# T5-bias attention into a bilinear feed-forward block on one NeuronCore: a reordered start of the queues, value rows of 160 bytes, and five more pairs of outputs transposed by DMA

## The chip, the cores and the metric

The kernel runs on one core of a Trainium2 chip. The metric is the device time of one execution in microseconds, as the median of several executions. A NeuronCore has five engines that each run their own instructions in order: TensorE (PE in the profile, its weight loads PEld), VectorE (DVE), ScalarE (ACT), GpSimd (POOL) and SyncE (SP), which here issues DMAs only. DMAs are issued by SP, ACT and GpSimd and run on the core's 16 DMA engines.

## The reference

```python
# q, k, v: 8 batches x 8 heads x 576 x 64, float32; bias_table: 32 buckets x 8 heads
scores = scale * np.matmul(q, k.transpose(0, 1, 3, 2))        # scale = 1/8
n = np.abs(pos[:, None] - pos[None, :])
bucket = np.where(n < 16, n, min(31, 16 + int(log(n / 16) / log(128 / 16) * 15)))
scores = scores + bias_table[bucket].transpose(2, 0, 1)
attn = softmax(scores);  y = attn @ v
x = y.transpose(0, 2, 1, 3).reshape(4608, 512)
out = ((x @ w_a) * (x @ w_b)) @ w_out                         # 512 -> 1536 -> 512
```

(The bucket's line is shortened here to one formula.) From a distance of 128 on all positions have bucket 31, so only a band around the diagonal has a bias that differs from a constant.

## The kernel before, in words

**Tiling.** Work goes by pairs of heads: pair p is heads 2(p mod 4) and 2(p mod 4)+1 of batch p // 4, 32 pairs in all. The 576 positions are four tiles of 128 and a tail of 64; the tails of both heads of a pair share one tile of 128 partitions (ktl, qtl, vt, with zeros in the other head's half). For each pair the kernel makes scores transposed, keys in the partitions: `qk1(p, t)` (L339) puts the scores of key tile t into one of the two PSUM buffers of pool ps_sc; `ex` (L350) takes the exponential on ScalarE into a tile `at`; `mul` (L358) multiplies the band by the exponential of the bias, from a table W per head pair, on VectorE. `qk_tail` (L364, L367, L370), `ex_tail` (L374 to L378) and `mul_tail` (L384, L387) do the same for the tail, with the tables Wt and W. `av(p, jq)` multiplies by the values: one matmul of 130 columns with the value tails vt (L400), then eight of 65 columns with the value rows vm (L409). The 65th column of a value row is 1, so that column gives the softmax's denominator. `norm` (L417, L418) divides and writes the output tile XG[p % 2].

**The bias.** The bias enters as a factor, the exponential of its difference to the constant of bucket 31, by head and distance. Its 8 rows are made in SBUF (tab_sb), written to DRAM (bias_tab) by a DMA on SP's queue (L222), and read back as W (`load_w`, L167) and Wt (L227), in which each partition has the row shifted by one place. For that reason W and Wt can't be loaded before that write has landed.

**Transposes.** For the first two batches q and k are transposed on TensorE: pairs 0 to 2 from float32 tiles (`t32`), pairs 3 to 7 from bf16 tiles qn and kn (`t_q` L291, `t_k` L311 and L303), each followed by a copy from PSUM (`c_q`, `c_k`, L255 on ScalarE or L257 on VectorE). From batch 2 on they are transposed by DMA on SP's queue (`turn`, L326 and L331). The output XG is transposed into xn, the input of the feed-forward block, by `t_x`: for the pairs from XD = 8 on, but the last, by two DMAs on SP's queue (L433, L436), for the others by five TensorE transposes (L442) and two copies (`c_x`, L257).

**PSUM.** Besides the two score buffers there is one bank for av, one (tag tr) that `t_q`, `t_k`, `t_x`, the tail's score tile qktt and the second part of av share, and two (tag ffn) for the feed-forward block and a few of the start-up's transposes. A bank is free again when its reader, a copy or norm, is done.

**Feed-forward block.** 4608 tokens are nine chunks of 512: one for each batch's main tiles and a ninth for all tails. A chunk is 36 units of four matmuls of 512 columns: `ff_a` (L464, with the copy L468), `ff_b` (L474, product L477) 12 times each, and 12 parts of `ff_o` (L484, copy L488, output DMA). wa and wb come in six parts each, wo in one DMA.

**Order.** The pools are under a manual schedule: every engine executes in the order in which the program issues. Pairs 0 to 3 are the start-up loop `for s in range(4)`, attention alone. From s = 4 on a list `steps` mixes the scores of pair s, the values of pair s - 1 and units of the feed-forward block, where the mark U stands for a place for units; `quotas` gives the number per pair (7, 7, 7, 6, 6, then 9).

**Queues.** SP has at the start: the first q and k pairs, kt and qt (the tails in float32, `load_pad`, L146), the bias table's write, pair 2 of q and k, W0, two Wt loads, W1, W2, W3. GpSimd's queue carries everything that is cast to bf16: values, qn, kn, tails, and the weights of the feed-forward block (`load_t` L124, `load_h`; `load_w_in` L159; `load_w_out` L164), with memsets of the zero halves and the ones between them (`pad`, `ones`). Each queue issues in order. A DMA uses one of eight semaphores in turn, so its issue also waits until the one eight before it has landed.

Of the kernel before, what the change touches and what calls it, by code (L numbers as in the profile page):

```python
# [13 lines left out]
def kernel(  # L14
# [11 lines left out]
    nc = tc.nc  # L26
# [34 lines left out]

    NR = 256
    TB = 512
    n_arr = np.abs(np.arange(NR) - NR // 2)
    half = NB // 2
    is_small = n_arr < half
# [30 lines left out]
    kn = [wpool.tile([128, H * NM * Dh], BF16, name=f"kn{i}") for i in range(2)]  # L97
    qtl = [wpool.tile([128, H, 2, Dh], BF16, name=f"qtl{i}") for i in range(2)]
    ktl = [wpool.tile([128, H, 2, Dh], BF16, name=f"ktl{i}") for i in range(2)]
    vm = [wpool.tile([128, H, NM, Dh + 1], BF16, name=f"vm{i}") for i in range(2)]  # L100
    vt = [wpool.tile([128, H, 2, Dh + 1], BF16, name=f"vt{i}") for i in range(2)]
    QTb = [wpool.tile([128, NM, H // 2, 128], BF16, name=f"QTb{i}") for i in range(2)]
    KTb = [wpool.tile([128, NM, H // 2, 128], BF16, name=f"KTb{i}") for i in range(2)]
    QTt = [wpool.tile([128, H // 2, 128], BF16, name=f"QTt{i}") for i in range(2)]
# [49 lines left out]
    def load_vt(b, nb):  # L154
        load_pad(nc.gpsimd, v, vt[b // 2 % 2], b, nb)
# [36 lines left out]
    nc.vector.memset(zero_sb[:, :], 0.0)  # L192
    pad(nc.vector, kt32, Dh)
    pad(nc.vector, qt32, Dh)
    load_pad(nc.sync, k, kt32, 0, 1)
    load_pad(nc.sync, q, qt32, 0, 1)
    nc.vector.memset(tab_sb[0:H, 0:127], 1.0)
    nc.vector.memset(tab_sb[0:H, 127 + NR:TB], 1.0)
    nc.vector.tensor_copy(out=id32[:, :], in_=ident)
    pad(nc.gpsimd, vt[0][:, 0:4, :, :], Dh + 1)  # L200
    ones(nc.gpsimd, vt[0][:, 0:4, :, :])
    for i in range(2):
        nc.vector.memset(vm[i][:, :, :, Dh:Dh + 1], 1.0)
        nc.vector.memset(att_sb[i][:, 1088:1152], 0.0)
    nc.vector.tensor_tensor(out=bt_sb[0:NB, :], in0=bt_sb[0:NB, :], in1=bl_sb[0:NB, :],
                            op=mybir.AluOpType.subtract)

# [6 lines left out]

    warm_up(7)
    nc.scalar.activation(out=eb_sb[0:NB, :], in_=bt_sb[0:NB, :], func=ACTF.Exp)
    tps = ps_av.tile([128, 512], FP32, tag="av", name="tab_ps")
    nc.tensor.matmul(out=tps[0:H, 0:NR], lhsT=eb_sb[0:NB, :], rhs=cst[0:NB, 128:128 + NR],
                     start=True, stop=True)
# [1 line left out]
    nc.vector.tensor_copy(out=tab_sb[0:H, 127:127 + NR], in_=tps[0:H, 0:NR])  # L221
    nc.sync.dma_start(out=tab.ap(), in_=tab_sb[0:H, :])  # L222
    load32(2, q, q32, (nc.sync, nc.sync))
    load32(2, k, k32, (nc.sync, nc.sync))
    load_w(nc.sync, 0)
    for hh in range(2):
        nc.sync.dma_start(out=Wt_sb[64 * hh:64 * hh + 64, :, :],  # L227
                          in_=bass.AP(tensor=tab, offset=hh * TB + 192,
# [2 lines left out]

    load_vp(0, 0)
    load_vt(0, 1)
    load_p(q, qn, 0, 3)
    load_p(k, kn, 0, 3)
    load_vp(0, 1)
    load_t(v, None, 0, 4, 8)
    load_w_in(0)
    for x in (ktl, qtl):
        pad(nc.gpsimd, x[0][:, 4:8, :, :], Dh)  # L240
    load_tails(1, 1)
    load_t(q, qn, 1, 0, 8)
    load_t(k, kn, 1, 0, 8)
    load_w_in(1)
    pad(nc.gpsimd, vt[0][:, 4:8, :, :], Dh + 1)
    ones(nc.gpsimd, vt[0][:, 4:8, :, :])
    load_vt(1, 1)
    load_v(1)
    load_w_in(2)
# [139 lines left out]
    def av(p, jq, where=AV):  # L389
        b, hp = divmod(p, 4)  # L390
        i = b % 2
        s = st[p]
        if jq == 0:
            s["rc"] = wrk.tile([128, 5, 2], FP32, tag="rc", name=f"rc{p}")
        if jq in (0, 3):
            s["pav", jq] = where[0].tile([128, 3, 2, Dh + 1], FP32, tag=where[1], name=f"av{p}_{jq}")
        pav, slot = s["pav", 3 * (jq // 3)], jq % 3
        att = att_sb[p % 2]
        x = att[:, 1024:1152] if jq == 4 else att[:, 512 + 128 * jq:640 + 128 * jq]
        nc.tensor.matmul(out=pav[:, slot, :, :], lhsT=x, rhs=vt[b // 2 % 2][:, 4 * i + hp, :, :],  # L400
                         start=True, stop=True)
        for hh in range(2):
            for t in range(NM):
                if jq < 4:
                    x = s["at", t][:, hh, 128 * jq:128 * jq + 128]
                else:
                    o = 256 * hh + ST * t
                    x = att[:, o:o + 128]
                nc.tensor.matmul(out=pav[:, slot, hh, :], lhsT=x,  # L409
                                 rhs=vm[i][:, 2 * hp + hh, t, :], start=False,  # L410
                                 stop=True, skip_group_check=True)

    def norm(p, j0):
# [5 lines left out]
            out=xg[:, j0:j0 + n, :, :], in0=pav[:, 0:n, :, 0:Dh],  # L419
            in1=rc.unsqueeze(3).to_broadcast([128, n, 2, Dh]), op=MULT)  # L420

    XD = 8

    def xc(b):
        o, u = SM * (b % 3), 3 * SM + ST * b
# [2 lines left out]
    def t_x(p, where=None):  # L428
        b, hp = divmod(p, 4)
        xg = XG[p % 2]  # L430
        main, rest = xc(b)
        if XD <= p < NP - 1:
            nc.sync.dma_start_transpose(  # L433
                out=xn_sb[hp][:, main].rearrange("d (t p) -> d t p", t=NM),
                in_=xg[:, 0:4, :, :].rearrange("p j a d -> p (j a d)"))
            nc.sync.dma_start_transpose(  # L436
                out=xn_sb[hp][:, rest].unsqueeze(1),
                in_=xg[0:64, 4, :, :].rearrange("p a d -> p (a d)"))
            return
        ps = bank(where, BF16, f"trx{p}")  # L440
        for jq in range(5):
            nc.tensor.transpose(ps[:, 128 * jq:128 * jq + 128], xg[:, jq, :, :], ident)  # L442
        st[p]["x"] = ps

    def c_x(p, eng=None):
        b, hp = divmod(p, 4)
        if XD <= p < NP - 1:
# [117 lines left out]
    for s in range(4):  # L565
        ex(s, 0)
        if s > 0:
            mul(s - 1, 3)
            mul_tail(s - 1)
        q_next(s)  # L570
        if s > 1:
            t_x(s - 2, FF)
        qk1(s, 2)
        ex(s, 1)
        if s > 1:
            c_x(s - 2)
        k_next(s)
        qk1(s, 3)
        ex(s, 2)
        if s == 0:  # L580
            tails_next(0, 2, None)
        else:
            tails_next(s + 1, 1, None)
        if s > 0:
            av(s - 1, 0)
            av(s - 1, 1)
        qk_tail(s)
        mul(s, 0)
        if s < 2:
            gate(s + 2)  # L590
        mul(s, 1)
        ex(s, 3)
        if s > 0:
            av(s - 1, 2)
            norm(s - 1, 0)
            av(s - 1, 3, FF)
        if s < 3:
            qk1(s + 1, 0)
        ex_tail(s)
        mul(s, 2)  # L600
        if s > 0:
            av(s - 1, 4)
            norm(s - 1, 3)
        if s < 3:
            qk1(s + 1, 1)
        if s == 2:
            load_w_in(3)
            load_w_in(4)
            load_w_in(5)
            load_t(q, qn, 2, 0, 8)  # L610
            load_t(k, kn, 2, 0, 8)
            for x in (ktl, qtl):
                pad(nc.gpsimd, x[1], Dh)
            load_tails(2, 2)
            load_w_out()
# [6 lines left out]

    def turns(s):
        b = s // 4 + 1
        if 2 <= b < B:
            i = s % 4 - (b == 2)
            if 0 <= i < 3:
                turn(b, "qkt"[i])

    quotas = {4: 7, 5: 7, 6: 7, 7: 6, 8: 6}  # L630
    for s in range(4, NP + 1):
# [3 lines left out]
        N = lambda j: (lambda: norm(s - 1, j))  # L635
        steps = []
        if s == 4:
            steps += [lambda: mul(3, 3), lambda: mul_tail(3), lambda: t_x(2, FF), lambda: c_x(2),
                      A(0, 1, 2), N(0), A(3, 4), N(3), lambda: t_x(3, FF), lambda: c_x(3), U,
                      lambda: t_q(4, TR), lambda: c_q(4, ACT), U, lambda: t_k(4, TR), lambda: c_k(4), U,  # L640
                      lambda: qk1(4, 0), lambda: ex(4, 0), lambda: qk1(4, 1), lambda: ex(4, 1), U,
                      lambda: qk1(4, 2), lambda: ex(4, 2), lambda: mul(4, 0),
                      lambda: qk1(4, 3), lambda: ex(4, 3), lambda: mul(4, 1), U,
                      lambda: qk_tail(4), lambda: ex_tail(4), lambda: mul(4, 2),
                      lambda: t_q(5, TR), lambda: c_q(5), U, lambda: mul(4, 3),
                      lambda: t_k(5, TR), lambda: c_k(5), lambda: mul_tail(4), U]
        elif new:
            e = early((s + 1) // 4)
            steps += [lambda: qk(s, 0), lambda: ex(s, 0), U, lambda: ex(s, 1), A(0, 1, 2), N(0), U,
                      lambda: mul(s, 0), A(3, 4), N(3)]  # L650
            if s > XD:
                steps += [lambda: t_x(s - 1), lambda: turns(s)]
            if e:
                steps += [lambda: t_q(s + 1, TR), lambda: c_q(s + 1)]
            steps += [U, lambda: mul(s, 1), lambda: qk(s, 2), lambda: ex(s, 2), U, lambda: ex(s, 3)]
            if e:
                steps += [lambda: t_k(s + 1, TR), lambda: c_k(s + 1)]
            steps += [U, lambda: mul(s, 2), U, lambda: mul(s, 3),
                      lambda: qk_tail(s), lambda: ex_tail(s), U]
            if s <= XD:  # L660
                steps += [lambda: t_x(s - 1, TR), lambda: c_x(s - 1), lambda: turns(s)]
            steps += [U, lambda: mul_tail(s), U]
        else:
# [57 lines left out]
```

The softmax here doesn't subtract the row's maximum and nothing guards it: scores larger than these inputs give would overflow.

## Time and profile before

| what | value |
|---|---|
| median of 12 runs | 433.55 us (432.57 to 434.47) |
| the profiled execution | 433.9 us, its span 432.1 |
| TensorE busy | 414.7 us, 96% of the span |
| ScalarE, VectorE, GpSimd busy | 241.6, 196.0, 118.1 us |
| first feed-forward unit (pa), first output unit (po) | 38.51 us, 77.97 us |
| DMA moved | 42.13 MB in 174055 packets; GpSimd's ring 66.0%, that of SP and ACT 30.8% of 16 engines' span |

Times in the text are microseconds from the start of the span if they name a moment. The span runs from the first to the last instruction on the profiled core; 1.8 us of the execution's own time lie outside it.

### The profile page before, as it was taken

How to read it: one execution, taken by the hardware profiler on the slowest of the kernel's cores; microseconds unless marked ns; L12 is line 12 of the kernel's file. 1: busy time of each engine (PE TensorE's matmuls, PEld its weight loads, DVE VectorE, ACT ScalarE, POOL GpSimd, SP SyncE). 2: the span in 40 equal slices, each digit the busy share in tenths (PEclk: the TensorE clock that was granted, in tenths of full speed). 3: DMA queues.
4: the chain of work that ended last, by engine and by line, in shares of the span. 5: the costliest groups of instructions: out<-in, count | busy, mean ns of one | idle time of the engine just before them, and what ended most of it. 6: DMA issues, size and time to landing. Idle time of an engine off the chain costs nothing.

```text
span 432.1 us, 8367 instructions
## 1 busy us (share of the span) xinstructions
PE 414.7 (96%) x3350; PEld 204.3 (47%) x3350; DVE 196.0 (45%) x482; ACT 241.6 (56%) x340; POOL 118.1 (27%) x164
## 2 busy tenths in 40 slices
PE   8678898999999999999999999999999999999995
PEld 3355454554445544444444455444444454444442
DVE  4395566535553455245534553355435541321320
ACT  3574766666665776666656675666566633223321
POOL 8989693583018100920073003000000000000000
PEclk9899999999999999999999999999999999999999
DMA  9999999999909990999099908931021001002004
GB/s 152 192 181 177 178 161 178 145 147 152 118 15 127 166 129 14 104 193 137 15 78 185 159 16 53 177 69 27 24 77 39 15 26 76 0 12 87 0 2 97
DMA packets 174055, 42.13 MB, mean 98 GB/s; under 512 B 160568, under 2 KB 169408, under 8 KB 174016
## 3 DMA queue, kind: packets, MB, share of 16 engines
q0 software_dynamic: 113296, 17.97, 66.0%
q1 hardware_dynamic: 59520, 23.27, 30.8%
q8 instruction: 26, 0.43, 0.4%
q10 hardware_dynamic: 1200, 0.36, 0.4%
q14 instruction: 13, 0.11, 0.1%
HBM read 38.83 MB, written 9.45 MB: 112 GB/s over the span
## 4 chain that ended last, share of the span: by engine, by line
PE 89%; DMA 4%; DVE 3%; ACT 1%; SPq 1%; issue 1%; ACTq 0%; DVEq 0%
PE pb L474 23%; PE po L484 22%; PE pa L464 22%; PE av L409 9%; PE qk L339 7%; PE av L400 2%; DMA Wt<-bias_tab 2%; PE qkt L364 1%; PE qkt L367 1%; DMA bias_tab<-tab_sb 1%; DVE XG L418 1%; DMA k<-in_k_dram 1%; ACT at L350 1%; DVE at L358 1%; SPq L146 1%
## 5 line engine op out<-in xcount | busy, mean ns | idle before, releaser
L350 ACT ACTIVATE at<-qk 128x1024 bf16<-128x1024 f32 x128 | 125.9, 1024 | 23.8 <-PE qk L339 23.8
L477 DVE TENSOR_TENSOR g<-pb,ha 128x512 bf16<-128x512 f32 x108 | 74.7, 692 | 125.9 <-PE pb L474 104.0
L464 PE MATMUL pa<-xn,wa 128*128 128x512 bf16 x432 | 111.1, 379 | 0.0
L474 PE MATMUL pb<-xn,wb 128*128 128x512 bf16 x432 | 110.9, 379 | 0.0
L468 ACT ACTIVATE ha<-pa 128x512 f32<-128x512 f32 x108 | 64.6, 598 | 77.2 <-PE pa L464 77.2
L484 PE MATMUL po<-wo,g 128*128 128x512 bf16 x432 | 102.5, 379 | 0.0
L358 DVE TENSOR_TENSOR at<-at,W 128x512 bf16<-128x512 bf16 (+1 forms) x128 | 60.2, 484 | 14.6 <-ACT at L350 10.0
L474 PEld LDWEIGHTS <-wb 128*128 128x128 bf16 x432 | 38.6, 97 | 53.1 <-issue 18.0
L464 PEld LDWEIGHTS <-wa 128*128 128x128 bf16 x432 | 38.8, 98 | 49.3 <-issue 10.3
L484 PEld LDWEIGHTS <-g 128*128 128x128 bf16 x432 | 38.5, 98 | 46.2 <-issue 7.6
L488 ACT ACTIVATE ob<-po 128x512 f32<-128x512 f32 x36 | 21.5, 597 | 69.0 <-PE po L484 69.0
L124 POOL DMA_DIRECT2D vm<-in_v_dram x32 | 27.6, 878 | 111.0 <-PE av L409 110.8
L409 PE MATMUL av<-vm,at 128*128 128x65 bf16 x1024 | 47.4, 194 | 0.0
L409 PEld LDWEIGHTS <-at 128*128 128x128 bf16 x1024 | 42.6, 98 | 7.0 <-issue 0.2
L417 DVE RECIPROCAL rc<-av 128x6 f32<-128x6 f32 x64 | 12.1, 188 | 53.4 <-PE av L409 53.4
L400 PE MATMUL av<-vt,att 128*128 128x130 bf16 x160 | 35.1, 219 | 0.1
L418 DVE TENSOR_TENSOR XG<-av,rc 128x384 bf16<-128x384 f32 x64 | 31.4, 491 | 2.8 <-DVE rc L417 0.7
L378 ACT ACTIVATE att<-qkt 128x1024 bf16<-128x1024 f32 x32 | 32.7, 1021 | 0.0
L339 PE MATMUL qk<-QTb,KTb 64*128 64x512 bf16 x192 | 29.1, 381 | 0.0
L124 POOL DMA_DIRECT2D kn<-in_k_dram x28 | 24.9, 904 | 14.6 <-DMA vt<-in_v_dram 5.2
L124 POOL DMA_DIRECT2D qn<-in_q_dram x28 | 24.8, 913 | 12.3 <-PE qk L339 7.3
L400 PEld LDWEIGHTS <-att 128*128 128x128 bf16 x160 | 15.8, 98 | 7.3 <-issue 0.7
(98 smaller groups left out, 215.7 us busy)
## 6 DMA issues: line engine op xcount, KB each, us to landing
out_dram<-ob SPq DMA_DIRECT2D x32, 256.0 KB, 4.2
qn<-in_q_dram POOLq DMA_DIRECT2D x28, 128.0 KB, 9.9
kn<-in_k_dram POOLq DMA_DIRECT2D x28, 128.0 KB, 13.2
vm<-in_v_dram POOLq DMA_DIRECT2D x28, 128.0 KB, 6.1
wa<-in_moe_w_a_dram POOLq DMA_DIRECT2D x6, 256.0 KB, 7.3
wb<-in_moe_w_b_dram POOLq DMA_DIRECT2D x6, 256.0 KB, 8.1
wo<-in_moe_w_out_dram POOLq DMA_DIRECT2D x1, 1536.0 KB, 14.9
out_dram<-ob SPq DMA_DIRECT2D x8, 128.0 KB, 2.3
```

Of the source, the lines that this page charges most:

```text
L124: nc.gpsimd.dma_start(out=(vm[b % 2][:, h0:h1, t, 0:Dh] if dst is None else dst[b % 2][:, :].rearrange("p (t h d) -> p t h d", h=H, t=NM)[ ...
L339: nc.tensor.matmul(out=ps[:, hh, :], lhsT=kT_(p, t)[r, :], rhs=qT[r, :, :], start=True, stop=True)
L350: nc.scalar.activation(out=at[:, :, :], in_=ps[:, :, :], func=ACTF.Exp, scale=scale)
L358: nc.vector.tensor_tensor(out=at[:, :, lo:hi], in0=at[:, :, lo:hi], in1=w[:, :, y:(None if z < 0 else z):-1], op=MULT)
L400: nc.tensor.matmul(out=pav[:, slot, :, :], lhsT=x, rhs=vt[b // 2 % 2][:, 4 * i + hp, :, :], start=True, stop=True)
L409: nc.tensor.matmul(out=pav[:, slot, hh, :], lhsT=x, rhs=vm[i][:, 2 * hp + hh, t, :], start=False, stop=True, skip_group_check=True)
L418: nc.vector.tensor_tensor(out=xg[:, j0:j0 + n, :, :], in0=pav[:, 0:n, :, 0:Dh], in1=rc.unsqueeze(3).to_broadcast([128, n, 2, Dh]), op=MULT)
L464: nc.tensor.matmul(out=pa[:, :], lhsT=wa_sb[df // FW][:, mc, 128 * (df % FW):128 * (df % FW) + 128], rhs=xn_sb[mc][:, xin(c)], start=(mc = ...
L468: nc.scalar.activation(out=ha[:, :], in_=pa[:, :], func=ACTF.Copy)
L474: nc.tensor.matmul(out=pb[:, :], lhsT=wb_sb[df // FW][:, mc, 128 * (df % FW):128 * (df % FW) + 128], rhs=xn_sb[mc][:, xin(c)], start=(mc = ...
L477: nc.vector.tensor_tensor(out=g_sb[df][:, :], in0=pb[:, :], in1=ff["ha"][:, :], op=MULT)
L484: nc.tensor.matmul(out=po[:, :], lhsT=g_sb[df][:, 128 * tt:128 * tt + 128], rhs=wo_sb[:, df, :], start=(df == 0), stop=(df == NDF - 1))
```

## The change

It has six parts.

1. The kt loads go from SP's queue to ACT's, behind the exponential of the table. On SP, W0 is loaded ahead of pair 2 of k.
2. On GpSimd all memsets of vt[0], ktl[0] and qtl[0] are issued before the first load, those of vt[1] ahead of batch 2's tails and wo (before: in the midst of pair 4). The values of pair 1 are loaded ahead of qn and kn of pair 3.
3. The rows of vm and vt are 80 elements (160 bytes) apart, not 65 (130 bytes); 65 are used as before.
4. XD is a set: pairs 0, 1, 4, 5 and 6 are transposed by DMA too, pairs 2, 3, 7 and 31 still on TensorE. The copies of the start-up's tail transposes for pairs 2 and 3, and of output pair 2, go from VectorE to ScalarE.
5. In the steps of pair 4 a place for units goes between qk(4,2) and qk(4,3), `t_q(5)` is issued ahead of `qk_tail(4)`, and no unit follows `t_k(5)`. In those of pairs 5 and 6 `t_q` of the next pair is issued behind `qk(s, 2)` and `qk(s, 3)`.
6. The DMA transposes of batch 2 are issued in the steps of pair 5 (q and k) and 6 (tails), before in those of pairs 5, 6 and 7.

```diff
+    VW = 80
...
-    vm = [wpool.tile([128, H, NM, Dh + 1], BF16, name=f"vm{i}") for i in range(2)]
-    vt = [wpool.tile([128, H, 2, Dh + 1], BF16, name=f"vt{i}") for i in range(2)]
+    vm = [wpool.tile([128, H, NM, VW], BF16, name=f"vm{i}") for i in range(2)]
+    vt = [wpool.tile([128, H, 2, VW], BF16, name=f"vt{i}") for i in range(2)]
...
-    load_pad(nc.sync, k, kt32, 0, 1)
     load_pad(nc.sync, q, qt32, 0, 1)
...
-    pad(nc.gpsimd, vt[0][:, 0:4, :, :], Dh + 1)
-    ones(nc.gpsimd, vt[0][:, 0:4, :, :])
...
+    pad(nc.gpsimd, vt[0], Dh + 1)
+    ones(nc.gpsimd, vt[0])
+    for x in (ktl, qtl):
+        pad(nc.gpsimd, x[0], Dh)
...
     nc.scalar.activation(out=eb_sb[0:NB, :], in_=bt_sb[0:NB, :], func=ACTF.Exp)
+    load_pad(nc.scalar, k, kt32, 0, 1)
...
     load32(2, q, q32, (nc.sync, nc.sync))
+    load_w(nc.sync, 0)
     load32(2, k, k32, (nc.sync, nc.sync))
-    load_w(nc.sync, 0)
...
     load_vt(0, 1)
+    load_vp(0, 1)
     load_p(q, qn, 0, 3)
     load_p(k, kn, 0, 3)
-    load_vp(0, 1)
...
-    for x in (ktl, qtl):
-        pad(nc.gpsimd, x[0][:, 4:8, :, :], Dh)
     load_tails(1, 1)
...
-    pad(nc.gpsimd, vt[0][:, 4:8, :, :], Dh + 1)
-    ones(nc.gpsimd, vt[0][:, 4:8, :, :])
...
-    XD = 8
+    XD = {0, 1, 4, 5, 6} | set(range(8, NP - 1))
...
-        if XD <= p < NP - 1:
+        if p in XD:
...
-            tails_next(s + 1, 1, None)
+            tails_next(s + 1, 1, ACT)
...
+        if s > 0:
+            av(s - 1, 4)
         mul(s, 2)
         if s > 0:
-            av(s - 1, 4)
             norm(s - 1, 3)
+        if s in (1, 2):
+            t_x(s - 1)
...
             load_t(k, kn, 2, 0, 8)
+            pad(nc.gpsimd, vt[1], Dh + 1)
+            ones(nc.gpsimd, vt[1])
             for x in (ktl, qtl):
                 pad(nc.gpsimd, x[1], Dh)
             load_tails(2, 2)
...
-            i = s % 4 - (b == 2)
-            if 0 <= i < 3:
-                turn(b, "qkt"[i])
+        if b == 2:
+            for x in {5: "qk", 6: "t"}.get(s, ""):
+                turn(b, x)
...
-                      lambda: qk1(4, 2), lambda: ex(4, 2), lambda: mul(4, 0),
-                      lambda: qk1(4, 3), lambda: ex(4, 3), lambda: mul(4, 1), U,
-                      lambda: qk_tail(4), lambda: ex_tail(4), lambda: mul(4, 2),
-                      lambda: t_q(5, TR), lambda: c_q(5), U, lambda: mul(4, 3),
-                      lambda: t_k(5, TR), lambda: c_k(5), lambda: mul_tail(4), U]
+                      lambda: qk1(4, 2), lambda: ex(4, 2), lambda: mul(4, 0), U,
+                      lambda: qk1(4, 3), lambda: ex(4, 3), lambda: mul(4, 1), lambda: t_q(5, TR),
+                      lambda: c_q(5), U, lambda: qk_tail(4), lambda: ex_tail(4), lambda: mul(4, 2), U,
+                      lambda: mul(4, 3), lambda: t_k(5, TR), lambda: c_k(5), lambda: mul_tail(4)]
...
-            if s > XD:
+            if s - 1 in XD:
                 steps += [lambda: t_x(s - 1), lambda: turns(s)]
+            steps += [U, lambda: mul(s, 1), lambda: qk(s, 2), lambda: ex(s, 2)]
             if e:
                 steps += [lambda: t_q(s + 1, TR), lambda: c_q(s + 1)]
-            steps += [U, lambda: mul(s, 1), lambda: qk(s, 2), lambda: ex(s, 2), U, lambda: ex(s, 3)]
+            steps += [U, lambda: ex(s, 3)]
...
-            if s <= XD:
+            if s - 1 not in XD:
                 steps += [lambda: t_x(s - 1, TR), lambda: c_x(s - 1), lambda: turns(s)]
...
         if s == 4:
-            pad(nc.gpsimd, vt[1], Dh + 1)
-            ones(nc.gpsimd, vt[1])
-            for x in (ktl, qtl):
-                pad(nc.gpsimd, x[0][:, 0:4, :, :], Dh)
+            pass
```

More of the change, by code (lines that the diff above doesn't have):

```diff
@@ L399, in av @@
         x = att[:, 1024:1152] if jq == 4 else att[:, 512 + 128 * jq:640 + 128 * jq]
-        nc.tensor.matmul(out=pav[:, slot, :, :], lhsT=x, rhs=vt[b // 2 % 2][:, 4 * i + hp, :, :],
+        nc.tensor.matmul(out=pav[:, slot, :, :], lhsT=x, rhs=vt[b // 2 % 2][:, 4 * i + hp, :, 0:Dh + 1],
                          start=True, stop=True)
@@ L409, in av @@
                 nc.tensor.matmul(out=pav[:, slot, hh, :], lhsT=x,
-                                 rhs=vm[i][:, 2 * hp + hh, t, :], start=False,
+                                 rhs=vm[i][:, 2 * hp + hh, t, 0:Dh + 1], start=False,
                                  stop=True, skip_group_check=True)
@@ L446, in c_x @@
         b, hp = divmod(p, 4)
-        if XD <= p < NP - 1:
+        if p in XD:
             return
@@ L570 @@
         q_next(s)
-        if s > 1:
-            t_x(s - 2, FF)
         qk1(s, 2)
         ex(s, 1)
-        if s > 1:
-            c_x(s - 2)
         k_next(s)
@@ L624, in turns @@
         b = s // 4 + 1
-        if 2 <= b < B:
-            i = s % 4 - (b == 2)
-            if 0 <= i < 3:
-                turn(b, "qkt"[i])
+        if b == 2:
+            for x in {5: "qk", 6: "t"}.get(s, ""):
+                turn(b, x)
+        elif 2 < b < B and s % 4 < 3:
+            turn(b, "qkt"[s % 4])
     quotas = {4: 7, 5: 7, 6: 7, 7: 6, 8: 6}
@@ L637 @@
         if s == 4:
-            steps += [lambda: mul(3, 3), lambda: mul_tail(3), lambda: t_x(2, FF), lambda: c_x(2),
+            steps += [lambda: mul(3, 3), lambda: mul_tail(3), lambda: t_x(2, FF), lambda: c_x(2, ACT),
                       A(0, 1, 2), N(0), A(3, 4), N(3), lambda: t_x(3, FF), lambda: c_x(3), U,
```

## The prediction

> **What bounds the kernel now.** I read the busy table by stretches first, because the share of the whole span mixes a start-up with a long steady part. Its columns after the engine's name are busy us and the count of instructions.
>
> ```profile
> 0.00:38.50 38.50, 29.23 (x309) 17.40 (x310) 22.74 (x75) 21.52 (x27) 34.25 (x58) 0.96 1.81 174
> 38.50:77.97 39.47, 35.88 (x336) 18.75 (x335) 22.80 (x56) 24.77 (x35) 26.05 (x39) 1.00 1.66 173
> 77.97:432.10 354.13, 349.59 (x2708) 168.13 (x2706) 150.41 (x351) 195.26 (x280) 57.83 (x69) 1.00 0.81 81
> ```
>
> TensorE is idle 9.3 us before the first FFN unit, 3.6 us from there to the first output unit at 77.97, and 4.5 in the remaining 354. So after 77.97 only fewer or shorter matmuls help. The chain that ended last says the same:
>
> ```profile
> PE 89%; DMA 4%; DVE 3%; ACT 1%; SPq 1%; issue 1%; ACTq 0%; DVEq 0%
> ```
>
> The chain cut to the start-up (start, length, what) shows what precedes it: the bias table's write to DRAM, then the two Wt loads from it.
>
> ```profile
> 7.80 5.42 DMA bias_tab<-tab_sb
> ...
> 14.33 6.84 DMA Wt<-bias_tab
> ...
> 21.60 0.68 DVE QT L257
> ```
>
> In VectorE's timeline the first multiplication by W waits 4.67 us for W0 (landed 18.93); that comes before the Wt wait. In TensorE's, qktt of pair 1 waits for the copy that frees its PSUM bank, and later two transposes wait for the same bank, held until the output copies of the pair before are done:
>
> ```profile
> 19.02 0.91 DVE L358 TENSOR_TENSOR at<-at,W 128x512 bf16<-128x512 bf16 x2 [4.67 <-DMA W<-bias_tab]
> ```
>
> ```profile
> 22.34 0.22 PE L370 MATMUL qktt<-KT 128*128 128x64 bf16 x2 [1.08 <-DVE QT L257]
> ...
> 54.70 0.40 PE L291 MATMUL trq<-cst_sb,qn 128*128 128x128 bf16 x4 [0.74 <-DVE XG L418]
> ...
> 66.22 0.40 PE L291 MATMUL trq<-cst_sb,qn 128*128 128x128 bf16 x4 [1.11 <-DVE XG L418]
> ```
>
> Last, a deadline that does not bind yet. The list of DMA issues and TensorE's timeline:
>
> ```profile
> wo<-in_moe_w_out_dram POOLq DMA_DIRECT2D x1, 1536.0 KB, 14.9
> ```
>
> ```profile
> 77.97 1.03 PE L484 MATMUL po<-wo,g 128*128 128x512 bf16 x4
> ```
>
> wo is issued at 57.30, moves from 61.10 to 71.08, lands at 72.17. First use is 77.97, a slack of 5.8 us.
>
> **What the skill says.** The page DMA: Bandwidth & Descriptors, section Queues, rings and completion order, says that each DMA engine takes turns between the queue rows that have work, packet by packet. The trace agrees: in 2 us slices around 66 us, 307 packets of the SP/ACT rings ran beside 307 of GpSimd's. Section Issuing engines are not separate DMA queues of that page says that another issuing engine saves issue time alone; here both rings fill the same 16 engines (share 1.81 in the first row, more than one packet outstanding per engine). TensorE: Matmul & The Clock Gate, section Wait — 56ns, not 53.3ns?, gives N/2.4 + 2.5 ns between warm matmuls: 29.6 ns for 65 columns. The trace has 32.5 ns for these (L409), but 56.4 for 130 (L400) and 29 to 30 for 64 columns (L370). SBUF — State Buffer, the note on 16-byte lines in section Door 1: The DMA port swizzle, makes a crossing to a new line cost: a row of 130 bytes touches nine lines at either row distance, so no gain follows from it.
>
> **The change part by part**, each against the profiled execution (span 432.1, time 433.9, so 1.8 lie outside the span). That time is 0.35 above the median of 433.55.
>
> 1. *Start-up, SP and ACT queues.* The kt loads leave SP for ACT: two issues of about 0.65 us. The table's write was issued at 7.80; two issues fewer, and a wait for an earlier load's landing at 6.98 (each issue waits for the eighth before it), put it at 6.9. It took 5.42 behind kt and qt. Bounds are 2.3 (an undisturbed 128 KB output) and 5.42; I take 3.9: landed 10.8. W0 now goes ahead of the k loads of pair 2: it took 5.65 behind them; bounds 2.3 and 5.65, taken 4.0: lands 14.9 instead of 18.93. VectorE was ready at 14.35, so its 4.67 wait shrinks to about 0.5. ACT's queue loses 1.2 us between two small operations in which it waited anyway; kt lands near 10 instead of 11.44, earlier than its transposes want it. The k loads behind W0 land about 16.3 (before 16.85), 0.4 after TensorE wants them: taken as hidden, at worst 0.5. Wt follows the transfer ahead of it by 2.2 as before (18.93 to 21.17): 16.3 + 2.0 = 18.3, bounds 17.3 and 19.9. From Wt to qktt(1) is 1.17 as before: 19.45 instead of 22.34, **−2.9**.
> 2. *Start-up, work removed.* Outputs of pairs 0 and 1 go by DMA: 10 transposes of 56 ns (0.56 us of TensorE), and their VectorE copies (425 + 180 ns each pair, overlapped 0.52). Two KT copies of 0.41 and one output copy move to ACT, which is 56% busy here. **−0.6** by the transposes; the copies are taken as cover for the rest. First FFN unit: 38.51 − 3.5 = 35.0. New waits: norm(2,0) and norm(3,0) on VectorE must wait until the DMA has read XG. xn(0) is issued at about 23.3; a like transposing DMA lands 2.4 after alone, 4 to 6 in traffic: 27 to 29, norm(2,0) comes near 30. xn(1) 27.5, lands 31 to 33.4, norm(3,0) near 33.4. Behind it would be the multiplications of pair 3, then PV, then TensorE. Taken as nothing, up to +1.
> 3. *Steps of pairs 4 to 6.* In pair 4 a unit lies between qk(4,2) and qk(4,3), and t_q(5) is ahead of the tail scores: TensorE's waits of 0.52 and 0.58 go, qk(5,0) now follows t_k(5) directly and waits 0.7 for KT instead of 0.46: −0.86. In pairs 5 and 6 t_q(s+1) comes after a unit, so the waits of 0.74 and 1.11 go, 0.2 left of each: −1.45. Ten transposes of pairs 4 and 5: −0.56. Together **−2.9**: TensorE would reach the first output unit at 77.97 − 3.5 − 2.9 = 71.6.
> 4. *GpSimd queue: what is late next.* The memsets of vt[0], ktl[0], qtl[0] run before the first load (issued 5.6, was 3.45); the transfer ring was at its limit from 8.4 on, so 2.15 of delay is partly made up by what SP's ring takes meanwhile: +0.3, bounds −0.5 and +1.1. vt[1]'s memsets (1.33) now stand ahead of the tails' loads and wo, whose issue had 3.8 us in hand to its first packet: 0, bound +1.33. Three transposing DMAs (pairs 0, 1, 4) of 640 packets each take the engines 0.7 us a pair: +2.1, bound +3.6. wo lands at 72.17 + 2.4 = **74.6**, three us after TensorE wants it. So the first output unit moves to 74.6, −3.4 and not −6.4. The output and turn DMAs queued on SP follow by as much: KTb of batch 2 lands about 76 (78 at worst) against its qk at 77.4 + 0.6, KTt 80 against 84, the last value tails 84 against 88: hidden, though with little over.
> 5. *After it.* Five transposes of pair 6: **−0.28**. All matmul groups after are as before.
> 6. *Padding.* 1280 instructions change row distance from 130 to 160 bytes. If alignment were the excess of 2.9 ns, 1280 × 2.9 = −3.7; if rows at 160 were 2 ns dearer, +2.9. The spacing is 32.5 ns at every row, whether 130·i is a multiple of 4, 16 or neither, and reading has nine lines either way: **0**. Loads write 128 of every row's bytes; their packets took the same 32 ns into vm (130 bytes apart) as into qn (128).
>
> Sum: 433.9 − 3.4 − 0.28 = 430.2; off the median, **429.9**.
>
> **Rivals.** *wo is not late* (its packets start as before, 72.2): −5.8 − 0.28, 427.5. For it: 3.8 us between issue and first packet; against: that wait was the ring's backlog, which the new DMAs lengthen. *Padding pays*: −3.7 more, 426.2. Against: all alignments have one time. *Slower: the queue's delays add up.* One mechanism: wo is last on GpSimd's queue, and 2.15 (late start) + 1.33 (memsets) + 3 × 1.2 (the transposing DMAs taking turns packet by packet with the loads) = 7.1. Then wo lands at 79.3, the first output unit waits till there: +1.3 − 0.28, 434.6. It decides from 78.25 on, a delay of 6.1. For it: turns are shared one for one; against: the engines work without gap, so only work added ahead counts, 2.1. *No start-up gain* (table and Wt land as late as before): 71.6 + 2.9 = 74.5, hidden by wo: 429.9 as well; the change does then half of what it says. If XG's wait and the k loads cost 1.5 besides, 431.4.
>
> **How the numbers follow.** Likeliest, wo late by about 2.4 (delay 1 to 4): chance 0.5, 429.9, its own range 428.4 to 431.6. wo not late 0.14; padding in either of these 0.06; start-up gain lost and more, 431 to 432.7, 0.1; within 0.2% (432.7 to 434.4) 0.05; slower 0.15, which holds the summed delays and a padding that costs. 0.2%, 0.87 us, is about what a measurement of this kernel can tell. Range 425.8 to 434.0: it takes in the padding's gain and the threshold of the slower rival. Faster 0.8, same 0.05, slower 0.15.
>
> **What would show it.** After: W0's wait on VectorE below 1 us; first pa near 35; no trx for pairs 0, 1, 4 to 6; trq(6), trq(7) waiting under 0.3; L484's first instruction with a wait of some 3 us for wo, near 74.6; 32.5 ns between AV matmuls. Wrong, if first pa is above 37, if wo lands before 72 or after 78, if qk of pair 8 waits for KTb, or if the stretch after the first output unit differs from 354.1 by more than 0.5.

## The result, and the profile after

The changed kernel takes 439.85 us (median of 8 runs, 438.54 to 441.31) against 433.61 for the kernel before (32 runs): a ratio of 1.0146, 95% interval 1.0134 to 1.0158. The forecast was 429.9 in a range of 425.8 to 434.0, so it was wrong in sign. The profiled execution is the quickest of the 8 (438.54 us, span 436.8, 4.7 more than before). Medians below are over all executions of a kernel, but ratios leave out those that a lower granted clock made longer, so the two can differ.

First the stretches, cut at the first feed-forward unit and the first output unit of this kernel (busy us and count by engine, then clock, DMA share, GB/s):

```profile
0.00:39.64 39.64, 26.33 (x300) 16.61 (x300) 20.83 (x67) 22.40 (x31) 31.86 (x50) 0.94 1.77 162
39.64:82.21 42.57, 35.87 (x326) 18.13 (x325) 23.25 (x55) 25.76 (x35) 25.66 (x36) 0.94 1.74 168
82.21:436.80 354.59, 349.65 (x2702) 166.86 (x2702) 148.50 (x346) 194.33 (x278) 59.96 (x71) 0.99 0.79 83
```

The start-up is 1.1 us longer than before (38.50), the stretch to the first output unit is 3.1 longer (39.47), and the rest is 0.5 longer (354.13). TensorE is busy for 2.9 us less before the first unit (29.23 before) and yet starts it later. In the chain that ended last, DMA rose from 4% to 10%:

```profile
PE 85%; DMA 10%; POOL 1%; DVE 1%; issue 1%; ACT 0%; SPq 0%; ACTq 0%; DVEq 0%
```

TensorE's timeline has the three waits that make it (start, length, in brackets the idle time and what ended it):

```profile
18.16 1.08 PE L514 MATMUL trk<-id,k 128*128 128x128 f32 x4 [3.23 <-DMA k<-in_k_dram]
...
38.63 0.50 PE L441 MATMUL trx<-cst_sb,XG 128*128 128x128 bf16 x3 [2.91 <-DVE XG L417]
...
39.64 1.91 PE L463 MATMUL pa<-xn,wa 128*128 128x512 bf16 x4
...
82.21 1.89 PE L483 MATMUL po<-wo,g 128*128 128x512 bf16 x4 [5.93 <-DMA wo<-in_moe_w_out_dram]
```

Read from the top: pair 2 of k comes 3.2 us too late; the output of pair 1, which a DMA is still reading, holds up VectorE, and so TensorE; wo comes 5.9 us too late. After the second and the third wait the four matmuls of a unit take 1.9 us instead of 1.0: TensorE runs at a lower clock for a while, 0.88 in the mean from 82 to 100 us by the table of stretches, and 12% of these 17.8 us are 2.1 us. VectorE's timeline names what the second wait is for, a DMA that is still reading XG, and the list of DMA issues has wo at 19.0 us from issue to landing instead of 14.9:

```profile
38.02 0.56 DVE L417 TENSOR_TENSOR XG<-av,rc 128x384 bf16<-128x384 f32 x1 [2.66 <-DMA xn<-XG]
```

```profile
wo<-in_moe_w_out_dram POOLq DMA_DIRECT2D x1, 1536.0 KB, 19.0
```

wo was issued at 63.12 instead of 57.30 and landed at 82.17 instead of 72.17. The transposes of q for pairs 5 to 7 have no wait any more (0.58, 0.74 and 1.11 before).

### The profile page after: what moved, and what is told of

Same layout as the page of the kernel before. It is cut to its first block, busy times and chain, and to the rows that moved or that the text cites. A ratio compares the mean times of both kernels' runs of the same rounds, so it can differ in the third digit from the quotient of the medians.

```text
span 436.8 us, 8318 instructions
## 1 busy us (share of the span) xinstructions
PE 411.8 (94%) x3325; PEld 201.6 (46%) x3325; DVE 192.6 (44%) x468; ACT 242.5 (56%) x344; POOL 117.5 (27%) x156
## 4 chain that ended last, share of the span: by engine, by line
PE 85%; DMA 10%; POOL 1%; DVE 1%; issue 1%; ACT 0%; SPq 0%; ACTq 0%; DVEq 0%
PE po L483 22%; PE pb L473 22%; PE pa L463 21%; PE av L408 8%; PE qk L338 7%; DMA wo<-in_moe_w_out_dram 4%; DMA k<-in_k_dram 2%; DMA xn<-XG 2%; PE av L399 2%; PE qkt L363 1%; PE qkt L366 1%; DMA bias_tab<-tab_sb 1%; PE qktt L369 0%; DVE KT L256 0%; DVE at L357 0%
## 5 line engine op out<-in xcount | busy, mean ns | idle before, releaser
L483 PE MATMUL po<-wo,g 128*128 128x512 bf16 x432 | 104.1, 384 | 5.9 <-DMA wo<-in_moe_w_out_dram 5.9
L408 PE MATMUL av<-vm,at 128*128 128x65 bf16 x1024 | 45.5, 194 | 0.0
L408 PEld LDWEIGHTS <-at 128*128 128x128 bf16 x1024 | 41.3, 98 | 6.7
```

What stands on the lines that cost most here:

```text
L408: nc.tensor.matmul(out=pav[:, slot, hh, :], lhsT=x, rhs=vm[i][:, 2 * hp + hh, t, 0:Dh + 1], start=False, stop=True, skip_group_check=True)
L483: nc.tensor.matmul(out=po[:, :], lhsT=g_sb[df][:, 128 * tt:128 * tt + 128], rhs=wo_sb[:, df, :], start=(df == 0), stop=(df == NDF - 1))
```

## The experiments

**1. The padding alone**, on the kernel before.

```diff
+    VW = 80
-    vm = [wpool.tile([128, H, NM, Dh + 1], ...
+    vm = [wpool.tile([128, H, NM, VW], ...      # vt likewise; 65 columns are read as before
```

> The kernel before with the padding alone. In the changed kernel the spacing of 65-column AV matmuls is mostly 29 to 30 ns where before it was 32.5, and the 130-column one 60 where it was 56.4. Theory (the padding itself does this): 1280 x -2.5 + 160 x 3.7 = -2.6 us, 431.0, with the same spacings here. Rival (the spacing follows from something else in the changed kernel, or the rows cost the loads what they give): within 0.5 of 433.6.

431.66 us, ratio 0.9953 (0.9938 to 0.9968): a gain of 1.9, less than the 2.6 expected, but on the theory's side. In the trace a 65-column matmul follows the one before it after 29 ns in most places (32.5 in the mean before), and after 35 at one place of the group of eight; the 130-column one takes 60 instead of 56. The stretch after the first output unit shows the gain too, 352.42 instead of 354.13:

```profile
77.28:429.70 352.42, 347.89 (x2708) 166.41 (x2706) 150.42 (x351) 195.24 (x280) 57.67 (x69) 1.00 0.73 81
```

**2. The DMA transposes of outputs 0, 1, 4, 5, 6 alone**, on the kernel before.

```diff
-    XD = 8
+    XD = {0, 1, 4, 5, 6} | set(range(8, NP - 1))
...
+        if s in (1, 2):
+            t_x(s - 1)
```

> The kernel before with part 4's DMA transposes of outputs 0, 1, 4, 5, 6 alone; queue orders, memsets, steps and turns as before. Theory (these DMAs are the loss: they wait behind GpSimd's packets, hold XG, and push GpSimd's ring back by 3 us and more): VectorE waits for XG some 3 us before the first FFN unit, wo lands at 77 or later, 435.5 to 438. Rival (the loss comes from the memsets, the later start of GpSimd's queue and the earlier turns): wo lands before 75.5, time 432.5 to 433.6 since ten transposes less are on TensorE after 38.5.

442.2 us, ratio 1.017 (1.0123 to 1.0218), beyond what was expected. VectorE waits 2.44 for XG, the first feed-forward unit is at 40.97, and GpSimd's ring is 4.3 us late at 36 us. (A ring is the list of packets that a queue's DMAs still have to move. By the trace's packet records it is late by the time that it takes longer than in the kernel before to start the same number of packets.) wo lands at 76.9, but TensorE does not wait for it, as everything is later. Instead KTb, which on SP's queue is behind the outputs of pairs 4 and 5, lands at 87.80. TensorE's timeline:

```profile
40.30 0.34 PE L442 MATMUL trx<-cst_sb,XG 128*128 128x128 bf16 x3 [2.66 <-DVE XG L418]
...
87.85 0.61 PE L339 MATMUL qk<-QTb,KTb 64*128 64x512 bf16 x4 [3.31 <-DMA KTb<-kn]
```

**3. and 4. The changed kernel with these outputs back on TensorE**: all five, or 0 and 1 only.

```diff
-    XD = {0, 1, 4, 5, 6} | set(range(8, NP - 1))
+    XD = set(range(8, NP - 1))               # 3;  {4, 5, 6} | ... in 4
...
+        if s > 1:
+            t_x(s - 2, FF)       # with its copies, where it was before
```

> The changed kernel with outputs 0, 1, 4, 5, 6 back on TensorE (everything else of the change kept). Theory (the DMAs are the loss): no XG wait, first FFN unit near 36.5, wo lands near 76 and TensorE waits at most 3 us for it, with the padding's 2.6 the time is 428.5 to 431. Rival (memsets and late start are the loss): wo still lands after 79, 434 to 437.

430.7 us, ratio 0.9932 (0.9917 to 0.9947): wo lands at 76.77, and TensorE waits 1.46 for it. Only the first unit's place was missed, 39.06 and not 36.5.

> The changed kernel with outputs 0 and 1 alone back on TensorE; 4, 5, 6 stay on DMA. Theory (wo sets the end and lands later by what each transposing DMA adds): the first FFN unit comes near 36.5, the wait for xn's read is gone, but wo lands only some 3.2 earlier, near 79, and TensorE still waits 5 or more: 436 to 437. Rival (the held XG is the loss, wo only follows from it): wo below 77.5, 433 to 434.5.

428.74 us, ratio 0.9895 (0.9863 to 0.9926). Neither theory's number came. With pairs 0 and 1 off the DMAs wo lands at 74.3, 7.9 earlier than in the changed kernel, where the theory had counted 3.2. So without the DMAs of pairs 0 and 1 the rest of the change is a gain, and their cost grows on the way to wo. Those of pairs 4 to 6 gain 2.0 over experiment 3 by the medians. TensorE's timeline of experiment 4:

```profile
19.72 1.09 PE L514 MATMUL trk<-id,k 128*128 128x128 f32 x4 [4.38 <-DMA k<-in_k_dram]
...
74.37 1.04 PE L483 MATMUL po<-wo,g 128*128 128x512 bf16 x4 [0.18 <-DMA wo<-in_moe_w_out_dram]
```

The first line shows what is left in the start-up: pair 2 of k. The first unit is at 38.45, where it was in the kernel before (38.51).

**5. Three buffers of XG** in the changed kernel: all its DMAs, but nothing to hold.

```diff
-    XG = [wpool.tile([128, 5, 2, Dh], BF16, name=f"XG{i}") for i in range(2)]
+    XG = [wpool.tile([128, 5, 2, Dh], BF16, name=f"XG{i}") for i in range(3)]
...
-        xg = XG[p % 2]
+        xg = XG[p % 3]
```

> The changed kernel with three buffers of XG, so that no norm has to wait for the DMA that reads the pair before the last; all DMAs stay. Theory (two losses: the held XG stalls VectorE and then TensorE before the first FFN unit, and apart from that the transposing DMAs of pairs 0 and 1 push GpSimd's ring and so wo back): first FFN unit near 37.0 instead of 39.6, wo lands after 80 all the same, TensorE waits longer for it, 436.5 to 438.5. Rival (wo's lateness follows from the stall of the start-up): wo lands before 77.5, 432 to 434.

Its ten runs reach from 434.1 to 442.3 (median 438.19; ratio 1.0072, 1.0034 to 1.011). The wait for XG is gone and the first unit comes at 37.75, but GpSimd's ring is 5 us late as in the changed kernel, and in the profiled execution, one of the quickest (434.24), wo holds TensorE for 4.12:

```profile
78.25 1.89 PE L483 MATMUL po<-wo,g 128*128 128x512 bf16 x4 [4.12 <-DMA wo<-in_moe_w_out_dram]
```

So there are two losses, the held buffer and the ring; wo, which lands at 78.2, lies between what the two theories gave.

**6. The same DMAs without transposing** for outputs 0 and 1, whose transposes are left out.

```diff
+        if p < 2:
+            nc.sync.dma_start(out=xn_sb[hp][:, main].rearrange("d (t p) -> d t p", t=NM)[:, :, 0:120],
+                              in_=xg[:, 0:4, :, :].rearrange("p j a d -> p j (a d)")[:, :, 0:120])
+            nc.sync.dma_start(out=xn_sb[hp][:, rest], in_=xg[:, 4, 0, :])
+            return
```

(Left out: a memset on VectorE of the columns that are not copied.)

> The changed kernel, where the DMAs of outputs 0 and 1 copy without transposing: 512 packets of 240 bytes and 128 of 128 for each pair, instead of 640; 120 of every 128 columns. The transposes of these two outputs are left out. Theory (a transposing DMA halts all rings for about a us each time, beside its packets): no packet of 33 to 38 us takes over 500 ns, GpSimd's ring is 2 to 2.5 us behind the kernel before and not 4.7, VectorE's wait for XG under 1.5, wo lands at 75 to 77, 429 to 432. Rival (the copies queue behind GpSimd's packets, whatever they do): landing still 8 us after issue, 438 to 440.

432.26 us, five runs from 430.1 to 438.9, ratio 0.9924 (0.9902 to 0.9947). The trace is of the longest of them (438.85). From 33 to 39 us no packet of the two rings takes over 141 ns. In the changed kernel 113 packets take over 500 ns there, up to 1635 (18 to 60 is usual; the kernel before has two such packets, of 629 and 1100), and in the us from 37 to 38 GpSimd's ring starts 88 packets where 395 is its usual rate for those of 512 bytes. GpSimd's ring is 2.8 us late at 40 us, not 4.7, and the two DMAs of pair 1 land after 6.3 and 7.2 us instead of 8.8 and 8.5. So a part of the latency is queueing, but the pause of all rings comes with the transposing: about one us for each DMA, two DMAs for a pair. In this execution wo lands at 82.13 all the same, as late as in the changed kernel; experiment 13 comes back to that.

**7. Pair 2 of k ahead of W0**, with outputs 0 and 1 on TensorE (experiment 4).

```diff
-    load_w(nc.sync, 0)
     load32(2, k, k32, (nc.sync, nc.sync))
+    load_w(nc.sync, 0)
```

> The changed kernel with outputs 0 and 1 on TensorE (428.7), and pair 2 of k ahead of W0 on SP as before. Theory (behind W0 the k loads come 2 to 3 us too late, which TensorE waits for, and Wt gains nothing): k of pair 2 lands before 15.5, no wait above 1 us before its transposes, first FFN unit at 36.5 to 37.5 instead of 38.45; wo at 74 then sets the first output unit, 428.0 to 428.6. Rival (W0's early arrival is what the change gains): first FFN unit at 39 or later, 429.2 or more.

428.6 us, ratio 0.9887 (0.9853 to 0.9921), no faster than experiment 4 beyond their spread. But the first unit is at 34.92, 3.5 earlier, more than expected: k lands at 14.81, W0 at 16.0, Wt at 17.95, and at 50 us GpSimd's ring is level with the kernel before, where experiment 4 was 1.95 late. Then the wait for wo takes back most of it. TensorE's timeline:

```profile
34.92 1.05 PE L463 MATMUL pa<-xn,wa 128*128 128x512 bf16 x4
...
73.27 1.04 PE L483 MATMUL po<-wo,g 128*128 128x512 bf16 x4 [2.62 <-DMA wo<-in_moe_w_out_dram]
```

**8. Start as before**: experiment 4 with parts 1 and 2 undone (SP, ACT and GpSimd queues and all memsets).

> Outputs 0 and 1 on TensorE and every queue of the start and all memsets of GpSimd as before (parts 1 and 2 undone); padding, steps, turns and the DMAs of outputs 4 to 6 stay. Theory (parts 1 and 2 bring nothing, they cost GpSimd's ring 2 us): first FFN unit within 0.3 of 38.45, wo lands near 72.5 with no wait, 428.2 to 428.9. Rival (the new start hides a gain): first FFN unit at 39 or later, over 429.3.

427.58 us, ratio 0.9861 (0.9844 to 0.9878), with a spread of only 1.1 over its runs. GpSimd's ring is 1.1 us ahead of the kernel before; wo lands at 72.64, and the first output unit is at 73.50 without a wait. So parts 1 and 2 of the change are not needed for what the rest gains.

**9. and 10. wo in thirds, or wo ahead of memsets and tails**, both on experiment 7.

```diff
-        nc.gpsimd.dma_start(out=wo_sb[:, :, :], in_=moe_w_out.rearrange(...))     # 9
+        for i in range(3):
+            nc.gpsimd.dma_start(out=wo_sb[i][:, :, :], in_=moe_w_out[512 * i:512 * i + 512, :].rearrange(...))
```

```diff
+            load_w_out()                                                        # 10
             pad(nc.gpsimd, vt[1], Dh + 1)
...
             load_tails(2, 2)
-            load_w_out()
```

(Left out of 9: the three tiles, and their names in the matmuls that read them.)

> The kernel with outputs 0 and 1 on TensorE and pair 2 of k ahead of W0 (428.6), with wo loaded by three DMAs of 512 KB into three tiles, so that the first output unit needs the first third alone. Theory (the whole of wo landing at 73.27 is what holds the first output unit there, TensorE being ready at 70.65): first output unit at 70.7 to 71, the later thirds cost under 0.5, 2 to 2.6 less: 426.0 to 426.6. Rival (the unit waits for something else that ends near 73, or qk of pair 8 then waits for its turns): 427.5 or more.

427.21 us, ratio 0.9845 (0.9827 to 0.9862). That lies between the two theories. The profiled run is the longest of its five (429.53; the others 426.5 to 427.3). In it the first output unit is at 71.33 with no wait, but then TensorE waits 1.16 for the last third and 1.12 for KTb: there the wait has only moved on.

> The same kernel (428.6) with wo in one piece, but issued ahead of vt[1], ktl[1], qtl[1] memsets and batch 2's tails. Theory (the memsets and the 2048 packets of the tails ahead of wo delay it by 2 to 2.5): wo lands at 70.5 to 71.5, first output unit with a wait below 1, 426.0 to 427.0. Rival (wo then runs beside KTb instead of behind it and gains nothing, and the tails come late for QTt and KTt): wo lands at 73 or later, 428.5 to 431.

430.62 us, ratio 0.9939 (0.992 to 0.9959), the rival's number by another way. wo's last packets start at 68.0 and TensorE comes to its first output unit at 70.62 without a wait. But QTb, now beside wo, takes 16.0 us where it took 9.2 in experiment 7, KTb behind it is issued 2.9 later and lands at 77.03 instead of 75.44, and the first scores of pair 8 wait:

```profile
77.08 1.03 PE L338 MATMUL qk<-QTb,KTb 64*128 64x512 bf16 x4 [3.21 <-DMA KTb<-kn]
```

**11. The changed kernel with pair 2 of k ahead of W0**, all DMAs kept (the edit of experiment 7).

> The changed kernel with pair 2 of k ahead of W0 on SP as before, nothing else undone; outputs 0, 1, 4 to 6 by DMA. Theory (order of the k loads and the DMAs of pairs 0 and 1 are two losses that add): TensorE's 3.2 wait for k goes and GpSimd's ring is 2 us less behind, the XG wait stays; first FFN unit at 36 to 38, wo lands at 75 to 78, 431 to 435. Rival (the DMAs of pairs 0 and 1 are all of it): 438.5 or more.

434.54 us, ratio 1.0039 (1.0014 to 1.0063). The two losses add: in the profiled run, the quickest (432.47), the first unit is at 36.22, GpSimd's ring is 3.0 late at 50 us, and wo is 3.57 late. By the medians this one line of order is 5.3 of the changed kernel's 6.2 us. But the 20 runs reach from 432.5 to 440.1, so some are as long as those of the changed kernel. TensorE's and VectorE's timelines:

```profile
76.55 1.89 PE L483 MATMUL po<-wo,g 128*128 128x512 bf16 x4 [3.57 <-DMA wo<-in_moe_w_out_dram]
```

```profile
35.55 0.42 DVE L417 TENSOR_TENSOR XG<-av,rc 128x256 bf16<-128x256 f32 x1 [2.00 <-DMA xn<-XG]
```

**12. Experiment 9 with outputs 4 and 5 on TensorE too.**

```diff
-    XD = {4, 5, 6} | set(range(8, NP - 1))
+    XD = {6} | set(range(8, NP - 1))
```

(Left out: two lines that keep the turns of batch 2 in the steps of pairs 5 and 6.)

> The kernel with wo in thirds (427.2), with the outputs of pairs 4 and 5 on TensorE too, so that of the pairs before 8 only pair 6 goes by DMA; the turns of batch 2 stay where they are. Theory (each pair by DMA holds the rings back by 1.3 us and more, so without pairs 4 and 5 KTb and the last third of wo come before TensorE wants them): TensorE's waits of 1.16 and 1.12 there go, 0.56 of transposes comes back, 425 to 426.2. Rival (TensorE then waits as long for the bank of the transposes or for KTb): 427 or more.

430.42 us in the median: three runs from 426.1 to 427.5, three from 433.3 to 435.5 (ratio 0.9888, 0.9837 to 0.9938). In the profiled run, the shortest of all here (426.13), no wait for wo or KTb is left, as the theory has it. As half of its runs are longer, this can't be called better than experiments 8 and 9.

**13. Outputs 4 to 6 on TensorE, 0 and 1 on DMA**, turns as in the changed kernel.

```diff
-    XD = {0, 1, 4, 5, 6} | set(range(8, NP - 1))
+    XD = {0, 1} | set(range(8, NP - 1))
```

> The changed kernel with the outputs of pairs 4, 5 and 6 on TensorE; 0 and 1 stay on DMA, the turns of batch 2 stay where they are. Open is the second half of wo's lateness: at 58 us GpSimd's ring is 4.7 us behind the kernel before, but wo lands 10.0 later. Theory (pairs 4 to 6 and their pauses, ahead of wo and beside it, make the other 5): wo lands at 77 to 79, first output unit there, 434.5 to 437. Rival (the earlier turns of batch 2 make it, or the ring's delay alone): wo lands after 81, 439 or more.

437.76 us, 18 runs from 431.7 to 441.8, ratio 1.0044 (1.0016 to 1.0072). In the profiled one (433.32) GpSimd's ring is 5.3 late at 50 us, and wo's packets start at 69.2, 8.4 later than before; but they take 9.1 us and not the changed kernel's 13.6 (before: 10.8, from 60.82 to 71.58), and TensorE waits 0.48:

```profile
78.80 1.04 PE L483 MATMUL po<-wo,g 128*128 128x512 bf16 x4 [0.48 <-DMA wo<-in_moe_w_out_dram]
```

So without the outputs of pairs 5 and 6, which in the changed kernel are transposed beside wo, wo's transfer isn't long. For its later start beyond the ring's delay the turns remain: QTb and nearly all of KTb now come ahead of it. Its time doesn't tell the theories apart, as its runs lie on both sides.

The same DMAs don't always make wo's transfer long, though. SP's issues in the changed kernel and in experiment 5:

```profile
63.27 4.33 SPq L330 DMA_TRANSPOSE KTb<-kn  x1
67.69 1.34 SPq L432 DMA_TRANSPOSE xn<-XG  x1
```

```profile
64.41 7.83 SPq L330 DMA_TRANSPOSE KTb<-kn  x1
72.33 2.57 SPq L432 DMA_TRANSPOSE xn<-XG  x1
```

In the changed kernel over half of KTb's packets (1138 of 2048) have gone when wo's start at 68.08, and the output of pair 5 is issued at about that moment. In the profiled executions of experiments 5 and 11 none of them have gone, KTb moves beside wo, the output of pair 5 is issued 5 to 6 us after wo's start, and wo's packets take 10.6 and 11.1 us. In that of experiment 6, 850 of KTb's have gone, pair 5 comes as in the changed kernel, and wo's take 15.4. So the last part of wo's lateness goes with which of two transfers starts first. The prediction had no term for that.

## Why the prediction was wrong, step by step

The profiled execution is 8.3 us above the sum's 430.2. Nearly all of it, 7.6, is there at the first output unit (82.21 instead of 74.6), and 0.7 comes after it.

**Step 1, start-up queues: the k loads were mis-sized, and with them Wt.** Table and W0 came about as worked out (landed 10.41 and 15.43; 10.8 and 14.9 forecast). The loads of pair 2 of k behind W0 were put at 16.3, hidden "at worst 0.5"; they landed at 18.03 and TensorE waited 3.23. (In experiments 3, 4, 5 and 13, which have the same order, it waited 3.5 to 4.4.) Wt was put at 18.3 with 19.9 as the bound and landed at 20.42. The packet records of the changed kernel have both rings slow from 12.8 to 14.0 us, while W0 is read; why is not shown. Experiment 7 has about the forecast's numbers, 17.95 for Wt and 34.92 for the first unit (forecast 18.3 and 35.0), with the two loads the other way round: the 3.5 us were there, and the order that was to bring them was the one that lost them.

**Step 2, the held XG: named, but priced at nothing.** xn(1) was issued at 29.15, not 27.5, and landed after 8.8 us, where 4 to 6 was taken; VectorE waited 3.0 in all, TensorE 2.91, and the clock fell. "Up to +1" had the path right (PV, then TensorE) and the size wrong by three. Experiment 5 takes the hold away and gets the first unit 1.9 earlier; the order of step 1, put back in experiment 11, gets it 3.4 earlier. The 4 to 6 were also read too short. In the trace of before the first of these DMAs, issued at 94.97, 96.22 and 106.64 for pairs 8 and 9, took 7.9, 7.3 and 8.3 us, and tile xn's view has that longest one:

```profile
DMA to landing us min/median/max: 2.3/3.4/8.3
```

**Step 3, the order of pairs 4 to 6: right.** In experiment 4 the stretch between the first unit and the first output unit is 35.92 with 0.18 of waiting, 3.55 below before. The padding has 0.17 of that (experiment 1: 39.30), so 3.4 where 2.9 was forecast.

**Step 4, wo: right path, wrong size, and this step decided the sign.** The sum was +2.4; it was +10.0. This is the step that failed: a pair's transposing DMAs were counted by their packets, 0.7 us. In the packet records GpSimd's ring lost 2.5 us to pair 1, since around each of the two DMAs all rings pause for about one us: experiment 6 shows the pauses gone when nothing is transposed. The order of W0 and k, which was given no cost on this ring, went with about 2 us of its delay (experiment 4 against 7). vt[1]'s memsets, put at 0, are on the chain now, as GpSimd stood in front of them only at 56.80. The chain of the changed kernel, cut to 55 to 90 us:

```profile
55.89 0.88 POOL kn L125
...
56.80 0.54 POOL vt L177
...
58.30 0.52 POOL ktl L177
...
63.12 19.04 DMA wo<-in_moe_w_out_dram
```

A ring that is 4.7 late at 55 us then met the turns and the outputs of pairs 5 and 6, and 4.7 became 10.0: wo's packets start 7.3 late (68.08) and take 2.8 longer. The rival that ends slower had this path (late start, memsets, DMAs in turn, wo past 78.25), with 7.1 us and a chance of 0.15; it knew nothing of the pauses either, and ended at 434.6. What was held against it, that only added packets count, was the error. The Trainium skill (DMA: Bandwidth & Descriptors, section Queues, rings and completion order) has the engines take turns packet by packet, and the trace of before agrees with 307 packets beside 307. The 0.7 us rested on that, and it leaves out that all rings can stand still, as they do here.

**Steps 5 and 6.** The five transposes of pair 6 are gone. The padding was taken as 0 and gives 1.9 (experiment 1), inside its bounds. Of the nine 16-byte lines that were to be touched either way nothing follows: the spacing fell to 29 ns, about the 29.6 that the prediction worked out for 65 columns. "32.5 ns at every row" was a misreading: it is a mean. In the trace of before, the rows whose distance 130·i from the tile's start is a multiple of 16 (every eighth, the first of each group of eight) are followed after 29 ns, the ones behind them after 35, the others after 32 to 33. Half of those first rows are at a multiple of 32 and half are not, with the same 29, so 32 isn't what they need. Whether it is the start of a row or its place in the group can't be told apart, and no run varies it. After the first output unit the padding's 1.7 (354.13 to 352.42) and the 0.28 are about what the lower clock costs (2.1); in the end that stretch is 0.5 longer.

**What was not settled:** why the runs of one kernel spread by 8 to 10 us in experiments 5, 6, 11, 12 and 13. The order of KTb and wo (experiment 13) may be a part of it: the long run that was profiled in experiment 6 (438.85) has the changed kernel's order, with TensorE waiting 6.67 us for wo, and the quick ones of experiments 5 and 11 have the other. That is three traces, and what sets the order was not tried.

## What to carry to other kernels

Count a moved transfer by what it does to the queue it shares, not by its bytes: here two small transposing DMAs each for pairs 0 and 1, off every critical path by their own size, delayed by 7.9 us (82.2 against 74.3) a load issued 34 us later, and the engine that waited for it then also lost clock. A load at the end of a full ring needs its slack checked against everything that is added ahead of it and beside it. Of the change the parts that shorten TensorE's own work and waits are worth keeping: padding, the order of pairs 4 to 6 and outputs 4 to 6 by DMA, with the start as before, take 427.58 us (ratio 0.9861, 0.9844 to 0.9878). With the new start, k ahead of W0 and wo in thirds it is 427.21 (0.9845, 0.9827 to 0.9862), which can't be told apart from that.

## What the runs showed of the hardware that was not expected

- Beside a DMA that transposes, the packets of GpSimd's and SP's rings paused for about one us: packets that take 18 to 60 ns took up to 1635 (changed kernel, 33 to 39 us), at most 141 with plain copies in their place (experiment 6). It isn't so beside every such DMA. In the trace of before, those of output pair 8 (issued at 94.97 and 96.22) landed after 7.9 and 7.3 us without one packet over 500 ns meanwhile, but around batch 3's turn of q 21 packets, from 91 to 93 us, took up to 1469. What makes the difference is not shown.
- A matmul of 65 columns follows the one before it after 29 ns in most places with value rows 160 bytes apart, after 32.5 in the mean with 130 (experiment 1). A 130-column one over two such rows takes 60 instead of 56.
- After a wait TensorE may run at half speed for a while: a unit's four matmuls take 1.9 us instead of 1.0 after waits of 5.93, 2.91 (the changed kernel) and 2.17 us (experiment 11, first unit), but 1.04 after the 2.62 of experiment 7. The length alone doesn't decide. The traces' clock records halve the clock for 3.41 or 6.83 us at a time, always from a bound of a grid of 3.41 us, which lies differently in each run. Two tables of stretches show the grid's stretches around the wait for XG in the changed kernel, and around that for wo in experiment 7:

```profile
35.15:38.56 3.41, 0.57 (x18) 0.44 (x14) 0.74 (x3) 0.00 (x0) 0.89 (x2) 1.00 1.81 144
38.56:41.97 3.41, 3.02 (x14) 1.62 (x15) 1.05 (x5) 0.38 (x1) 3.09 (x5) 0.50 2.23 160
```

```profile
68.66:72.07 3.41, 1.99 (x24) 0.78 (x19) 2.56 (x7) 2.46 (x3) 0.00 (x0) 1.00 1.43 174
72.07:75.49 3.42, 2.22 (x15) 1.18 (x16) 0.18 (x1) 0.65 (x2) 0.88 (x1) 1.00 1.48 146
```

The wait of experiment 7 falls into two stretches, and TensorE is busy for over half of each (1.99 and 2.22 us); the wait in the changed kernel leaves 0.57 busy in one stretch, and the next has clock 0.50. In experiment 9 two waits of 1.16 and 1.12 us in one stretch were enough. So it is in all 15 traces up to 420 us: of about 1800 stretches at full clock, the 19 with TensorE busy for under 0.55 of them were followed by half clock, and of those with over 0.58 none was (of the three in between, at about 0.57, one was).
